# Pair 0's k by keys is transposed on TensorE, and the last 64 positions of k, q and v come in a load of their own

## The chip, the cores and the metric

The kernel runs on one core of one Trainium2 chip. Its time is device microseconds, from the first to the last instruction with what the device adds around them. A core has five engines, each with its own program: TensorE (PE, with its weight loads as PEld), VectorE (DVE), ScalarE (ACT), GpSimd (POOL) and SyncE (SP), which here issues nearly all transfers.

## The reference

Three stages follow each other: retention attention (32 heads, 576 positions, head size 64), a feed-forward layer with hard-swish, and one with SoLU and a layer norm.

```python
scores = scale * np.matmul(q, k.transpose(0, 1, 3, 2))      # (4, 8, 576, 64)
gamma = 1.0 - 2.0 ** (-5.0 - np.arange(H))
Dmat = np.where(rel >= 0, gamma[:, None, None] ** rel[None, :, :], 0.0)
x = np.matmul(scores * Dmat, v)                             # then (2304, 512)
h = x @ w_in                                                # (512, 2048)
x = (h * np.clip(h + 3.0, 0.0, 6.0) / 6.0) @ w_out
h = x @ w2_in                                               # (512, 1024)
e = np.exp(h - h.max(-1)); solu = h * e / (e.sum(-1) + 1e-09)
ln = (solu - mean) / np.sqrt(var + 1e-06) * g_ln
out = ln @ w2_out                                           # (2304, 512)
```

## The kernel before

Attention works on pairs of heads, 16 in all, and within a pair on five chunks: four of 128 positions and a last one of 64. Because the decay is a power of the distance, only the diagonal 128x128 blocks of the scores are computed; everything older goes through a running state per chunk. For pair n the names in the trace are these.

- k and q transposed (head size on the partitions): rk, rq; k by keys (positions on the partitions): rn; v: rv. For the first three pairs all four are called raw (in the order's rows raw0_0 is k of pair 0, raw0_1 q, raw0_2 k by keys, raw0_3 v).
- s: the scores of the four full chunks (`scores`); st: these scaled by ACT and masked by POOL.
- z: the scores of the last 64 positions (`short`); st4: z times mask4, on DVE.
- v: rv scaled by the decay (`prep`), on ACT or DVE.
- u: k by keys times v (`chunk_states`), from which DVE sums the four states (state).
- xp: the output of a pair, from st and v (`values`) and from state and q (`short`); xa: xp times the table tab on DVE (`evac_x`).
- place: one matmul and copies on ACT and POOL that make tab.

In `kernel` the host lays k and q out as 576 columns, the last 64 of them with the two heads swapped, and v as nine rows per partition, of which the last holds the last 64 positions.

The first part of the program, up to the second layer's products, is not written in its final order. Each step is entered in a plan (`Plan`) with its engine, an estimate of its time, what it reads and what it writes. TensorE's steps keep the order in which they are entered. For the others the plan plays the program through, several times, and sets the order in which each engine's steps are issued, by due times and by estimates of engines and transfers (`LOOK`, `DMA_KB`, `HELD` and others); some elementwise steps may go to DVE instead of POOL or ACT. All of SP's transfers form one queue, issued in order.

At the start PE runs warm, nine matmuls on zeros (`N_WARM`), then s of pair 0, z, place, u of pair 0, s of pair 1, xp, z and u of pair 1, and so on. From pair 5 on a share of the first layer, h, stands between the pairs. Transfers of the first three pairs (`EARLY`) use buffers of later stages, those of the other pairs three or four buffers each (`PA`).

Of the kernel before, what the change touches and what calls it, by code (L numbers as in the profile page):

```python
# [9 lines left out]
F32 = mybir.dt.float32  # L10
# [26 lines left out]
WRAW = 2  # L37
EARLY = 3
NE = 4
N_WARM = 9  # L40
PRODUCTS = (
    ("a11", "b11"), ("a12", "b21"), ("s2", "t2"), ("s1", "t1"), ("s4", "b22"), ("s3", "t3"), ("a22", "t4"),
)
# [66 lines left out]
class Plan:  # L110


    LOOK, HOP, DMA_US, DMA_KB, DMA_ONE = 0.8, 0.2, 2.2, 375.0, 150.0
    DEEP, PASSES, YIELD, GAP, KEEP = 3.0, 5, 0.3, 5.0, 1e9
    HELD = ((3.0, 1.4), (23.0, 0.3))

    def __init__(self):
        self.ops, self.homes, self.last = [], {}, {}
# [135 lines left out]
    def simulate(self, nexts, free, loose=False):  # L254
# [51 lines left out]
        while len(begun) < len(self.ops):  # L306
            progress = True
            while progress:
                progress = False
                for e in engines:  # L310
                    if e in active or idle_at[e] > now:
                        continue
                    o = choose(e)
                    if o is None:
                        continue
                    waiting[o.engine].discard(o)
                    if o.engine != e:
                        o.engine, o.us, o.port = "DVE", o.alt[1], True
                    o.start = now
                    begun.append(o)  # L320
                    for v in starts[o]:
                        freed(v, now)
                    if e == "SP":
                        idle_at[e] = now + 0.1
                        begin = max(dma, now)
                        dma = begin + o.kb / self.DMA_KB
                        dma += sum(us for at, us in self.HELD if begin < at <= dma and not loose)
                        o.end = max(dma, now + o.kb / self.DMA_ONE) + self.DMA_US
                        ends.append(o)
# [24 lines left out]


@with_exitstack
def retention_hardswish_solu_kernel(ctx, tc, kt, qt, kn, vt, w1, w2i, w2o, gln, decay, place, out):


    nc = tc.nc  # L360
# [543 lines left out]
    def at_x(c):  # L904

        return slice(128 + CHUNKS[c].start, 128 + CHUNKS[c].stop)

    def load_pair(pr):

        if pr >= NPAIR:  # L910
            return
        early = pr < EARLY
        tag = "wi" if pr < 2 else "g"
        rk, rq, rn, rv = (
            buf("g" if i == 3 else tag, shape, f"raw{pr}_{i}") if early else abuf(name, shape, f"{name}{pr}")
            for i, (name, shape) in enumerate((
                ("rk", [128, S]), ("rq", [128, S + 128]), ("rn", [128, 512]), ("rv", [128, 9, D]),
            ))
        )
        move(288, lambda: sy.dma_start(out=rk(), in_=kt[pr]), (), (rk,))  # L920
        n = S if early else S + 128
        move(n / 2, lambda: sy.dma_start(out=rq()[:, :n], in_=qt[pr][:, :n]), (), ((rq, 0),))
        move(288, lambda: sy.dma_start(out=rv(), in_=vt[pr]), (), (rv,))
        move(256, lambda: sy.dma_start(out=rn(), in_=kn[pr]), (), (rn,))
        for h in range(2 if early else 0):
            def go(e, h=h):
                o, i = rq()[HEADS[h], S:], rq()[HEADS[1 - h], CHUNKS[3]]
# [6 lines left out]
        raws[pr] = rk, rq, rn, rv  # L934

    def prep(pr):

        if pr >= NPAIR:
            return
        rv = raws[pr][3]  # L940
        v = vs[pr] = abuf("v", [128, 9, D], f"v{pr}")
        p = pr % NP
        for i, (c0, n, at) in enumerate(((0, 4, 2 * p), (4, 4, 2 * p + 1), (8, 1, H + NP + p))):
            def go(e, c0=c0, n=n, at=at):
                o, i = (x()[:, c0:c0 + n].rearrange("p c d -> p (c d)") for x in (v, rv))
# [5 lines left out]
            either(0.3 if n > 1 else 0.15, 0.5 if n > 1 else 0.33, go, (rv,), ((v, i),), "ACT").earliest = 5.6  # L951

    def scores(pr):

        sp = [pbuf(f"s{h}", [128, 512], f"s{pr}_{h}") for h in range(2)]
        st = sts[pr] = [abuf(f"st{h}", [128, 512], f"st{pr}_{h}") for h in range(2)]
        k, q, _, _ = raws[pr]
        wide = pr <= A_FROM

        def go():  # L960
# [23 lines left out]
    def short(pr, now, old):  # L984
# [3 lines left out]
        if now:  # L988
            zp = pbuf("z", [128, 64], f"z{pr}")
            st4 = sts4[pr] = abuf("st4", [128, 64], f"st4{pr}")  # L990
            k, q, _, _ = raws[pr]
            reads, writes = [k, (q, 0)], [zp]
        first = pr > A_FROM
        if old:
            if first:
                xps[pr - 1] = pbuf("xp", [128, 1024], f"xp{pr - 1}")
            xp = xps[pr - 1]
            oq, v, state, ost4 = raws.pop(pr - 1)[1], vs[pr - 1], states.pop(pr - 1), sts4.pop(pr - 1)
            reads, writes = [*reads, oq, v, state, ost4], [*writes, xp]
# [536 lines left out]
    now = 0.0  # L1536
# [121 lines left out]
```

## Time and profile before

| | |
|---|---|
| median of 3 runs | 627.79 us (627.13 to 628.36) |
| profiled execution | 627.86 us, span 626.1 us |
| PE busy | 620.6 us, 99% |
| DVE, ACT, POOL busy | 464.2, 398.5, 313.5 us |
| moved by transfers | 145.77 MB, 233 GB/s over the span, 376 GB/s in the first 60 us |

The span is the time from the first to the last instruction; the 1.8 us beside it lie around the program. Busy time is the time in which an engine had an instruction under way. A wait is the idle time of an engine before an instruction, with what ended it behind the arrow. A record of a matmul runs into the next one's, so that start times say more than durations; a plain float32 matmul has two records.

### The profile page before, as it was taken

To read this page: it belongs to the slowest core of one execution; us is meant where nothing else is said; L and a number is where in the kernel's file an instruction comes from. 1 tells how busy PE (TensorE), PEld (TensorE's weight loads), DVE (VectorE), ACT (ScalarE), POOL (GpSimd) and SP (SyncE) were. 2 spreads that over 40 slices of the span, in tenths; PEclk is the share of its full clock that TensorE was granted. 3 is DMA by queue.
4 is the path that set the end of the run, shared out by engine and by line. 5 is a ranking of instruction groups with operands and counts; after the bars stand their busy time and mean duration, and the time that the engine had idled before them with its cause. 6 is when DMAs were issued, how large, how long until landed. Compare 5 with 4: busy or idle time off the path is not lost.

```text
span 626.1 us, 11161 instructions
## 1 busy us (share of the span) xinstructions
PE 620.6 (99%) x3999; PEld 518.6 (83%) x3999; DVE 464.2 (74%) x830; ACT 398.5 (64%) x690; POOL 313.5 (50%) x315
## 2 busy tenths in 40 slices
PE   8999999999999999999999999999999999999997
PEld 5878888988888888888888888888988888888887
DVE  4887999876788785798689888552878868778740
ACT  5887867956667551567566665421676876877672
POOL 6764733304344402572054230542578998999453
PEclk9999999999999999999999999999999999999999
DMA  9999987859667695745998669966665553344441
GB/s 325 394 391 397 408 305 264 294 195 329 203 211 245 209 321 189 294 167 185 379 309 307 222 215 389 383 254 195 175 189 129 118 90 96 102 101 85 84 113 56
DMA packets 91914, 145.77 MB, mean 233 GB/s; under 512 B 43858, under 2 KB 49746, under 8 KB 91860
## 3 DMA queue, kind: packets, MB, share of 16 engines
q1 hardware_dynamic: 91712, 145.06, 69.6%
q8 instruction: 31, 0.51, 0.3%
q14 instruction: 23, 0.19, 0.1%
q10 hardware_dynamic: 148, 0.02, 0.0%
HBM read 92.36 MB, written 43.25 MB: 217 GB/s over the span
## 4 chain that ended last, share of the span: by engine, by line
PE 96%; DMA 3%; SPq 0%; issue 0%; ACT 0%
PE acc L67 29%; PE h L67 23%; PE o L67 16%; PE sd L67 6%; PE sc L67 6%; PE sa L67 6%; PE sb L67 3%; PE xp L67 3%; PE x L67 2%; PE s L67 2%; DMA rn<-in_kn_dram 1%; PE u L67 1%; DMA rk<-in_kt_dram 1%; DMA raw<-in_qt_dram 1%; SPq L67 0%; PE z L67 0%
## 5 line engine op out<-in xcount | busy, mean ns | idle before, releaser
L67 PE MATMUL acc<-g,w1l 128*128 128x512 f32 x624 | 154.1, 389 | 0.0
L67 PEld LDWEIGHTS acc<-g,w1l 128*128 128x128 f32 x624 | 117.1, 188 | 24.3
L67 PE MATMUL o<-w,lt 128*128 128x512 f32 (+1 forms) x456 | 103.0, 378 | 0.0
L67 PEld LDWEIGHTS o<-w,lt 128*128 128x128 f32 x456 | 82.4, 188 | 16.3 <-POOL lt L67 0.4
L67 POOL TENSOR_TENSOR lt<-lT,lt 128x512 fp32r<-128x512 f32 x36 | 61.2, 1719 | 13.4 <-ACT lt L67 13.2
L67 ACT ACTIVATE e<-h,stat 128x1024 f32<-128x1024 f32 x36 | 41.3, 1148 | 35.1 <-DVE stat L67 35.1
L67 PE MATMUL h<-w2t,xt 128*128 128x512 f32 x216 | 53.5, 389 | 0.0
L67 PEld LDWEIGHTS h<-w2t,xt 128*128 128x128 f32 x216 | 40.3, 188 | 8.2
L67 PE MATMUL h<-x,w 128*128 128x512 f32 (+1 forms) x216 | 45.8, 361 | 0.0
L67 PE MATMUL acc<-g,w 128*128 128x512 f32 (+1 forms) x216 | 43.5, 354 | 0.0
L67 PEld LDWEIGHTS acc<-g,w 128*128 128x128 f32 x216 | 36.5, 189 | 6.1
L67 PEld LDWEIGHTS h<-x,w 128*128 128x128 f32 x216 | 34.9, 189 | 7.0 <-issue 1.7
L67 PE MATMUL h<-w2b,xt 128*128 128x512 f32 x162 | 39.8, 390 | 0.0
L67 ACT ACTIVATE wz<-wraw 128x512 f32<-128x512 f32 x44 | 29.4, 668 | 12.9 <-DMA wraw<-in_w2o_dram 5.0
L67 POOL TENSOR_TENSOR g<-gf,g 128x512 fp32r<-128x512 f32 (+1 forms) x18 | 24.1, 1336 | 26.3 <-ACT g L67 26.2
L67 DVE CUSTOM_DVE_ANT_0 wz<-wz,wt 128x1024 uint16<-128x1024 uint16 x44 | 35.2, 801 | 2.3 <-ACT wt L67 1.1
L67 DVE TENSOR_SCALAR e<-h,stat 128x1024 f32<-128x1024 f32 x18 | 20.5, 1142 | 21.0 <-POOL stat L67 21.0
L67 PEld LDWEIGHTS h<-w2b,xt 128*128 128x128 f32 x162 | 30.2, 188 | 6.1
L67 ACT ACTIVATE wt<-wraw 128x512 int32<-128x512 uint32 x48 | 31.9, 664 | 3.4 <-DMA wraw<-in_w2o_dram 1.0
L67 DVE CUSTOM_DVE_ANT_0 h<-h,h 128x512 f32<-128x512 f32 x36 | 24.7, 685 | 11.7 <-PE h L67 4.7
L67 DVE SCALAR_TENSOR_TENSOR h<-h,e 128x1024 f32<-128x1024 f32 x18 | 28.1, 1563 | 7.0 <-ACT e L67 7.0
L67 ACT ACTIVATE g<-gf 128x512 fp32r<-128x512 f32 (+1 forms) x44 | 26.4, 600 | 10.2 <-DVE gf L67 8.9
(193 smaller groups left out, 1359.6 us busy)
## 6 DMA issues: line engine op xcount, KB each, us to landing
w1l<-w1s SPq DMA_DIRECT2D x34, 512.0 KB, 6.0
wraw<-in_w_dram SPq DMA_DIRECT2D x32, 512.0 KB, 5.7
w1s<-w1o SPq DMA_DIRECT2D x10, 512.0 KB, 4.5
x2l<-x2s SPq DMA_DIRECT2D x18, 256.0 KB, 5.9
x2f<-x2o SPq DMA_DIRECT2D x18, 256.0 KB, 5.1
x2r<-x2f SPq DMA_DIRECT2D x9, 512.0 KB, 4.6
rq<-in_qt_dram SPq DMA_DIRECT2D x13, 352.0 KB, 6.5
out_dram<-osb SPq DMA_DIRECT2D x17, 256.0 KB, 2.0
```

Source lines behind the costliest of these rows:

```text
L67: return lambda *args, **kw: self.keep(op(*args, **kw))
```

## The change

The host no longer puts the last 64 positions at the end of k, q and v. They form an array of their own, rt, with 192 columns per pair: k, q and v of those positions. Each pair has one more load, of 96 KB, and its other loads have 256 or 320 KB instead of 288 or 352. z and the last chunk's part of xp read rt.

For pair 0 the load of k by keys goes. In its place PE transposes the four chunks of k by matmuls against a unit matrix, eye, into one bank (flip), and a copy on DVE or ACT brings it to the buffer that u reads. eye is made on POOL by a memset and two selects. The warm-up has six matmuls instead of nine, and three estimates of the plan are others.

```diff
-N_WARM = 9
+N_WARM = 6
...
-    HELD = ((3.0, 1.4), (23.0, 0.3))
+    HELD = ((3.0, 0.4), (5.2, 0.4), (12.5, 0.6))
...
-                        o.end = max(dma, now + o.kb / self.DMA_ONE) + self.DMA_US
+                        o.end = max(dma, now + o.kb / self.DMA_ONE if now > self.FRESH else 0.0) + self.DMA_US
...
+    eye = pa.tile([128, 128], F32, name="eye")
...
+    ge.memset(eye, 1.0)
+    for step in (1, -1):
+        ge.affine_select(
+            out=eye, in_=eye, compare_op=ALU.is_ge, fill=0.0, base=0, pattern=[[step, 128]], channel_multiplier=-step,
+        )
...
+    def flip(rk, rn):
+
+        kp = bank("flip", at=0)
+
+        def go():
+            for c in range(4):
+                te.matmul(kp()[:, CHUNKS[c]], rk()[:, CHUNKS[c]], eye, start=(c == 0), stop=(c == 3))
+
+        def copy(e):
+            if e is se:
+                se.activation(out=rn(), in_=kp(), func=ACTF.Copy)
+            else:
+                ve.tensor_copy(out=rn(), in_=kp())
+
+        pl.op("PE", 0.95, go, (rk,), (kp,))
+        either(V_US, A_US, copy, (kp,), (rn,), "ACT")
...
-        move(288, lambda: sy.dma_start(out=rk(), in_=kt[pr]), (), (rk,))
-        n = S if early else S + 128
+        move(256, lambda: sy.dma_start(out=rk(), in_=kt[pr]), (), (rk,))
+        n = 512 if early else 640
         move(n / 2, lambda: sy.dma_start(out=rq()[:, :n], in_=qt[pr][:, :n]), (), ((rq, 0),))
-        move(288, lambda: sy.dma_start(out=rv(), in_=vt[pr]), (), (rv,))
-        move(256, lambda: sy.dma_start(out=rn(), in_=kn[pr]), (), (rn,))
+        move(256, lambda: sy.dma_start(out=rv(), in_=vt[pr]), (), (rv,))
+        rt = abuf("rt", [128, 3, 64], f"rt{pr}")
+        move(96, lambda: sy.dma_start(out=rt(), in_=short_rows[pr]), (), (rt,))
+        if pr:
+            move(256, lambda: sy.dma_start(out=rn(), in_=kn[pr]), (), (rn,))
+        else:
+            flip(rk, rn)
...
-                    te.matmul(zp()[HEADS[h]], k()[HEADS[h], CHUNKS[4]], q()[HEADS[h], CHUNKS[4]], start=True, stop=True)
+                    te.matmul(zp()[HEADS[h]], rt()[HEADS[h], 0], rt()[HEADS[h], 1], start=True, stop=True)
...
-                (2, st[:, 1], rq[:, CHUNKS[2]]), (4, st[:, 3], rq[:, CHUNKS[4]]),
+                (2, st[:, 1], rq[:, CHUNKS[2]]), (4, st[:, 3], ort()[:, 1]),
```

On PE the order stays, but for the start: nine warm matmuls before, six and four flips now, the flips directly ahead of s of pair 0. Behind that, from the last matmul of s of pair 0 to the first of s of pair 1, PE's rows were these.

```order
L67 MATMUL s0_1_199<-raw0_1_169,raw0_0_167 128x128
L67 MATMUL z0_209<-raw0_1_169,raw0_0_167 64x64 x2
L67 MATMUL place_214<-place_row_144 128x512
L67 MATMUL u0_229<-v0_220,raw0_2_175 64x64 x8
L67 MATMUL s1_0_253<-raw1_1_182,raw1_0_179 128x128
```

And now:

```order
L67 MATMUL s0_1_209<-raw0_1_173,raw0_0_171 128x128
L67 MATMUL z0_224<-rt0_177 64x64 x2
L67 MATMUL place_230<-place_row_144 128x512
L67 MATMUL u0_241<-v0_221,raw0_2_217 64x64 x8
L67 MATMUL s1_0_258<-raw1_1_183,raw1_0_179 128x128
```

z reads rt, and u's second operand is the buffer that the copy of flip writes. On DVE, from the copy of a part of q of pair 0 to the first sum of the state of pair 0, the rows were these.

```order
L67 COPY raw0_1_169<-raw0_1_169 64x128
L67 TENSOR_TENSOR st40_218<-z0_209,mask4_149 128x64
L67 TENSOR_SCALAR v0_220<-raw0_3_171,decay_sb_143 128x256
L67 TENSOR_SCALAR v0_220<-raw0_3_171,decay_sb_143 128x64
L67 COPY state0_243<-u0_229 128x64
```

And now:

```order
L67 COPY raw0_1_173<-raw0_1_173 64x128
L67 COPY raw0_2_217<-flip_196 128x512
L67 TENSOR_SCALAR v0_221<-raw0_3_175,decay_sb_143 128x256
L67 TENSOR_TENSOR st40_234<-z0_224,mask4_149 128x64
L67 COPY raw1_1_183<-raw1_1_183 64x128 x2
L67 COPY state0_269<-u0_241 128x64
```

The copy of flip stands ahead of v; the small part of v went to ACT, and the copies of q of pair 1 came from ACT. On SP, the loads up to the ones that pair 4's u and pair 5's s read (kn of pair 4 is rn4, k of pair 5 rk5) were these.

```order
L67 DMA rq4_281<-in_qt_dram 128x704
L67 DMA rn3_302<-in_kn_dram 128x512
L67 DMA rk4_318<-in_kt_dram 128x576
L67 DMA wraw_338<-in_w1_dram 128x1024
L67 DMA rv4_359<-in_vt_dram 128x576
L67 DMA rq5_377<-in_qt_dram 128x704
L67 DMA rn4_397<-in_kn_dram 128x512
L67 DMA rk5_417<-in_kt_dram 128x576
```

And now:

```order
L67 DMA rn3_290<-in_kn_dram 128x512
L67 DMA rq4_313<-in_qt_dram 128x640
L67 DMA rt3_330<-in_rt_dram 128x192
L67 DMA rk4_342<-in_kt_dram 128x512
L67 DMA wraw_353<-in_w1_dram 128x1024
L67 DMA rv4_387<-in_vt_dram 128x512
L67 DMA rn4_400<-in_kn_dram 128x512
L67 DMA rt4_417<-in_rt_dram 128x192
L67 DMA rq5_421<-in_qt_dram 128x640
L67 DMA rk5_444<-in_kt_dram 128x512
```

rt of a pair stands behind rv or rq, and rn4 ahead of rq5 now. The rows of DVE, ACT, POOL and SP differ in places up to the last third of what the plan orders; behind that and in the part that is written out by hand they are the same.

## Rows read from the trace of the kernel before

**Rows 1.** The page: TensorE's busy time, share of the span, instructions.
```profile
PE 620.6 (99%) x3999; PEld 518.6 (83%) x3999; DVE 464.2 (74%) x830; ACT 398.5 (64%) x690; POOL 313.5 (50%) x315
```

**Rows 2.** Waits of PE, whole span: total us, times, longest.
```profile
PE warm L67 <- DVE idle L440: 1.4, 1, 1.4
PE s L67 <- DMA raw<-in_qt_dram: 0.6, 1, 0.6
PE u L67 <- DMA rn<-in_kn_dram: 0.3, 1, 0.3
```

**Rows 3.** Timeline of PE, 0 to 30 us: start, duration, out<-in, records.
```profile
4.96 1.16 PE L67 MATMUL s<-raw,raw 64*128 64x128 f32 x16
6.05 0.33 PE L67 MATMUL z<-raw,raw 64*64 64x64 f32 x4
6.31 1.12 PE L67 MATMUL place<-place_row 2*128 2x512 f32 x2
7.36 0.69 PE L67 MATMUL u<-v,raw 128*64 128x64 f32 x16
8.61 1.16 PE L67 MATMUL s<-raw,raw 64*128 64x128 f32 x16 [0.56 <-DMA raw<-in_qt_dram]
...
21.07 0.27 PE L67 MATMUL z<-rq,rk 64*64 64x64 f32 x1
...
22.17 0.69 PE L67 MATMUL u<-v,rn 128*64 128x64 f32 x16 [0.32 <-DMA rn<-in_kn_dram]
22.87 1.16 PE L67 MATMUL s<-rq,rk 64*128 64x128 f32 x16
```

**Rows 4.** The chain of waits, 0 to 60 us: start, duration, what.
```profile
3.13 5.34 DMA raw<-in_qt_dram
8.49 5.98 DMA rk<-in_kt_dram
14.48 7.55 DMA rn<-in_kn_dram
```

**Rows 5.** Timeline of SP's queue, 0 to 30 us: issue, duration of issuing.
```profile
0.80 0.38 SPq L67 DMA_DIRECT2D raw<-in_kt_dram  x1
...
16.12 0.33 SPq L67 DMA_DIRECT2D rk<-in_kt_dram  x1
...
22.84 0.33 SPq L67 DMA_DIRECT2D rq<-in_qt_dram  x1
```

**Rows 6.** Transfers: 10 to 20, 34 to 44 (two rows), 70 to 80 us.
```profile
DMA packets 1770, 3.97 MB, mean 397 GB/s; under 512 B 197, under 2 KB 197, under 8 KB 1769
...
DMA packets 1971, 3.96 MB, mean 396 GB/s; under 512 B 218, under 2 KB 474, under 8 KB 1969
...
xd<-xa SPq DMA_DIRECT2D x3, 64.0 KB, 5.5
...
DMA packets 1485, 4.07 MB, mean 407 GB/s; under 512 B 295, under 2 KB 591, under 8 KB 1483
```

**Rows 7.** Timeline of PE, short windows from 3.7 to 4.8 us.
```profile
3.48 0.63 PE L67 MATMUL warm<-idle 128*128 128x512 bf16 x1
...
3.91 0.96 PE L67 MATMUL warm<-idle 128*128 128x512 bf16 x3
...
4.27 0.60 PE L67 MATMUL warm<-idle 128*128 128x512 bf16 x2
```

**Rows 8.** Window 3.8 to 4.3 us: busy (records), granted clock, transfers' share, GB/s.
```profile
3.80:4.30 0.50, 0.50 (x3) 1.00 1.08 396
```

**Rows 9.** Transfers issued from 0.7 to 1 us: count, KB, us to landing.
```profile
raw<-in_kt_dram SPq DMA_DIRECT2D x1, 288.0 KB, 2.9
```

**Rows 10.** Timeline of POOL, 0 to 8 us.
```profile
0.80 1.44 POOL L443 MEMSET mask<- 64x64 f32 x8 [0.29 <-POOLq L1647]
2.32 0.90 POOL L445 TENSOR_SCALAR_AFFINE_SELECT mask<-mask 64x256 f32<-64x256 f32 x2
```

**Rows 11.** Timeline of DVE, 4 to 13 us.
```profile
4.84 0.22 DVE L67 COPY raw<-raw 64x128 f32<-64x128 f32 x1 [3.52 <-DMA raw<-in_qt_dram]
...
11.65 0.76 DVE L67 TENSOR_TENSOR xa<-xp,tab_sb 128x576 f32<-128x576 f32 x1 [1.74 <-PE xp L67]
```

More of the change, by code (lines that the diff above doesn't have):

```diff
@@ L110 @@
 class Plan:
-    LOOK, HOP, DMA_US, DMA_KB, DMA_ONE = 0.8, 0.2, 2.2, 375.0, 150.0
+    LOOK, HOP, DMA_US, DMA_KB, DMA_ONE, FRESH = 0.8, 0.2, 2.2, 375.0, 150.0, 2.0
     DEEP, PASSES, YIELD, GAP, KEEP = 3.0, 5, 0.3, 5.0, 1e9
-    HELD = ((3.0, 1.4), (23.0, 0.3))
+    HELD = ((3.0, 0.4), (5.2, 0.4), (12.5, 0.6))
     def __init__(self):
@@ L356, in retention_hardswish_solu_kernel @@
 @with_exitstack
-def retention_hardswish_solu_kernel(ctx, tc, kt, qt, kn, vt, w1, w2i, w2o, gln, decay, place, out):
+def retention_hardswish_solu_kernel(ctx, tc, kt, qt, kn, vt, short_rows, w1, w2i, w2o, gln, decay, place, out):
     nc = tc.nc
@@ L895, in retention_hardswish_solu_kernel @@
     idle_b = known("x2e", idle)
-    PA = {"rk": 3, "rq": 4, "rn": 3, "rv": 3, "v": 3, "st0": 2, "st1": 2, "state": 2, "st4": 2, "xa": 2}
+    PA = {"rk": 3, "rq": 4, "rn": 3, "rv": 3, "rt": 4, "v": 3, "st0": 2, "st1": 2, "state": 2, "st4": 2, "xa": 2}
     def abuf(tag, shape, name):
@@ L914, in load_pair @@
         rk, rq, rn, rv = (
-            buf("g" if i == 3 else tag, shape, f"raw{pr}_{i}") if early else abuf(name, shape, f"{name}{pr}")
+            buf("gf" if not pr and i == 2 else "g" if i == 3 else tag, shape, f"raw{pr}_{i}") if early else abuf(name, shape, f"{name}{pr}")
             for i, (name, shape) in enumerate((
-                ("rk", [128, S]), ("rq", [128, S + 128]), ("rn", [128, 512]), ("rv", [128, 9, D]),
+                ("rk", [128, 512]), ("rq", [128, 640]), ("rn", [128, 512]), ("rv", [128, 8, D]),
             ))
         )
-        move(288, lambda: sy.dma_start(out=rk(), in_=kt[pr]), (), (rk,))
-        n = S if early else S + 128
+        move(256, lambda: sy.dma_start(out=rk(), in_=kt[pr]), (), (rk,))
+        n = 512 if early else 640
         move(n / 2, lambda: sy.dma_start(out=rq()[:, :n], in_=qt[pr][:, :n]), (), ((rq, 0),))
-        move(288, lambda: sy.dma_start(out=rv(), in_=vt[pr]), (), (rv,))
-        move(256, lambda: sy.dma_start(out=rn(), in_=kn[pr]), (), (rn,))
+        move(256, lambda: sy.dma_start(out=rv(), in_=vt[pr]), (), (rv,))
[5 more added lines that the diff above has]
+            flip(rk, rn)
         for h in range(2 if early else 0):
             def go(e, h=h):
-                o, i = rq()[HEADS[h], S:], rq()[HEADS[1 - h], CHUNKS[3]]
+                o, i = rq()[HEADS[h], 512:], rq()[HEADS[1 - h], CHUNKS[3]]
                 if e is se:
@@ L933, in load_pair @@
             either(0.22, 0.28, go, ((rq, 0),), ((rq, 1 + h),), "ACT")
-        raws[pr] = rk, rq, rn, rv
+        raws[pr] = rk, rq, rn, rv, rt
     def prep(pr):
@@ L939, in prep @@
             return
-        rv = raws[pr][3]
+        _, _, _, rv, rt = raws[pr]
         v = vs[pr] = abuf("v", [128, 9, D], f"v{pr}")
@@ L944, in go @@
             def go(e, c0=c0, n=n, at=at):
-                o, i = (x()[:, c0:c0 + n].rearrange("p c d -> p (c d)") for x in (v, rv))
+                o = v()[:, c0:c0 + n].rearrange("p c d -> p (c d)")
+                i = rv()[:, c0:c0 + n].rearrange("p c d -> p (c d)") if n > 1 else rt()[:, 2]
                 if e is se:
@@ L949, in go @@
                     ve.tensor_scalar(out=o, in0=i, scalar1=decay_sb[:, at:at + 1], scalar2=None, op0=ALU.mult)
-            either(0.3 if n > 1 else 0.15, 0.5 if n > 1 else 0.33, go, (rv,), ((v, i),), "ACT").earliest = 5.6
+            either(0.3 if n > 1 else 0.15, 0.5 if n > 1 else 0.33, go, (rv if n > 1 else rt,), ((v, i),), "ACT").earliest = 5.6
     def scores(pr):
@@ L956, in scores @@
         st = sts[pr] = [abuf(f"st{h}", [128, 512], f"st{pr}_{h}") for h in range(2)]
-        k, q, _, _ = raws[pr]
+        k, q = raws[pr][:2]
         wide = pr <= A_FROM
@@ L990, in short @@
             st4 = sts4[pr] = abuf("st4", [128, 64], f"st4{pr}")
-            k, q, _, _ = raws[pr]
-            reads, writes = [k, (q, 0)], [zp]
+            rt = raws[pr][4]
+            reads, writes = [rt], [zp]
         first = pr > A_FROM
@@ L997, in short @@
             xp = xps[pr - 1]
-            oq, v, state, ost4 = raws.pop(pr - 1)[1], vs[pr - 1], states.pop(pr - 1), sts4.pop(pr - 1)
-            reads, writes = [*reads, oq, v, state, ost4], [*writes, xp]
+            (_, oq, _, _, ort), v, state, ost4 = raws.pop(pr - 1), vs[pr - 1], states.pop(pr - 1), sts4.pop(pr - 1)
+            reads, writes = [*reads, oq, ort, v, state, ost4], [*writes, xp]
         def go():
@@ L1010, in go @@
             for c, w, qc in (
-                (1, st[:, 0], rq[:, CHUNKS[1]]), (3, st[:, 2], rq[:, S:]),
-                (2, st[:, 1], rq[:, CHUNKS[2]]), (4, st[:, 3], rq[:, CHUNKS[4]]),
+                (1, st[:, 0], rq[:, CHUNKS[1]]), (3, st[:, 2], rq[:, 512:]),
+                (2, st[:, 1], rq[:, CHUNKS[2]]), (4, st[:, 3], ort()[:, 1]),
             ):
@@ L1602, in retention_hardswish_solu_kernel @@
     pb.release()
-_INS = ["kt", "qt", "kn", "vt", "w1", "w2i", "w2o", "gln", "decay", "place"]
+_INS = ["kt", "qt", "kn", "vt", "rt", "w1", "w2i", "w2o", "gln", "decay", "place"]
 def kernel(**inputs):
@@ L1614 @@
     kt, qt = (np.array(a.transpose(0, 2, 1).reshape(NPAIR, 2 * D, S)) for a in (k, q))
-    for a in (kt, qt):
-        a[:, :, 512:] = np.roll(a[:, :, 512:], D, axis=1)
-    qt = np.concatenate([qt, np.roll(qt[:, :, 384:512], D, axis=1)], axis=2)
+    rt = np.empty((NPAIR, 128, 3, 64), np.float32)
+    for i, a in enumerate((kt, qt)):
+        rt[:, :, i] = np.roll(a[:, :, 512:], D, axis=1)
+    kt, qt = kt[:, :, :512], np.concatenate([qt[:, :, :512], np.roll(qt[:, :, 384:512], D, axis=1)], axis=2)
     kn = k[:, :512].reshape(NPAIR, 2, 4, 128, D).transpose(0, 3, 2, 1, 4).reshape(NPAIR, 128, 512)
-    vt = np.empty((NPAIR, 128, 9, D), np.float32)
-    vt[:, :, :8] = v[:, :512].reshape(NPAIR, 2, 4, 128, D).transpose(0, 3, 1, 2, 4).reshape(NPAIR, 128, 8, D)
+    vt = v[:, :512].reshape(NPAIR, 2, 4, 128, D).transpose(0, 3, 1, 2, 4).reshape(NPAIR, 128, 8, D)
     for h in range(2):
-        vt[:, 64 * h:64 * h + 64, 8] = v[1 - h::2, 512:]
+        rt[:, 64 * h:64 * h + 64, 2] = v[1 - h::2, 512:]
     wi, wo, w2i, w2o = (
@@ L1644 @@
     place, decay = place.astype(np.float32), np.concatenate([over, step, last, np.roll(step, D, axis=0)], axis=1).astype(np.float32)
-    host = dict(kt=kt, qt=qt, kn=kn, vt=vt, w1=w1, w2i=w2i, w2o=w2o, gln=gln, decay=decay, place=place)
+    host = dict(kt=kt, qt=qt, kn=kn, vt=vt, rt=rt, w1=w1, w2i=w2i, w2o=w2o, gln=gln, decay=decay, place=place)
     nc = _bacc.Bacc("TRN2", target_bir_lowering=False, num_devices=1, dynamic_dma_scratch_size=1024)
```

## The prediction

> **What bounds the kernel now.** I read the page first: TensorE (PE) is busy 620.6 of 626.1 us [rows 1]. Then PE's waits over the whole span: three in all, 1.38 us before the first warm-up matmul, 0.56 us for pair 1's q and 0.32 us for pair 4's k by keys [rows 2]. So after about 23 us PE never waits, and whatever happens to the other engines later can only add time. The change can win inside the first 23 us alone, and there at most 0.56 + 0.32 = 0.88 us, unless the first score matmul itself starts sooner. The timeline of PE places both waits: s of pair 1 starts at 8.61; u of pair 4 stands directly before s of pair 5, which starts at 22.87 [rows 3].
>
> The chain of waits says what feeds PE there: transfers, 3.13 to 8.47, 8.49 to 14.47, 14.48 to 22.03, one behind the other [rows 4]. Each link begins when the link before it has landed. The order shows why: eight loads stand between the two, and SP does not issue a load before the one eight places ahead has landed. By the same count the landing of rk5 (pair 5's k) is bounded: the load eight places behind it, rq7, is issued at 22.84 [rows 5]. So s of pair 5, at 22.87, starts just when rk5 is there: the transfers and PE meet at that place, although no wait is shown. From there each pair also carries a share of h on PE, and PE falls behind the transfers.
>
> **The load of kn for pair 0 goes; the last 64 positions travel alone.** Up to rk5 the queue carries, before, three pairs of 1,120 KB, two of 1,184, wraw with 512, rq5 with 352 and rk5 with 288: 6,880 KB. After: 864 (pair 0) + 2 x 1,120 + 2 x 1,184 + 512 + 320 + 256 = 6,560 KB. 320 KB less at 397 GB/s [rows 6] is 0.83 us. Against it stand four more loads (five of rt, less one of kn). Each is 128 rows and, by the counts of packets, 16 more: 576 packets over 16 engines, 36 each. What a packet costs beside its bytes the trace gives only between bounds. Ten microseconds with 1,770 packets move 3.97 MB, ten with 1,485 move 4.07 MB: solved for a price per packet that is 12 ns. But ten with 1,971 packets, three 64-KB stores among them, move as much as those with 1,770: that makes it nothing [rows 6]. I take the middle, 6 ns: 36 x 6 = 0.22 us, between 0 and 0.43. The transfers thus let s of pair 5 start 0.83 - 0.22 = 0.61 us sooner (0.40 to 0.83), at 22.26.
>
> The new loads are waited for at z, which now reads rt. rt4 has 5,984 KB ahead of it and in it, against 6,592 for kn of pair 4, which landed at 22.03 [rows 4]: 608 KB, 1.57 us sooner, with the packets 20.7. z of pair 4 stands at 21.07 [rows 3] and would be due at 20.70 without waits (21.07 - 0.56 + 0.19, below). It just arrives; a tenth late here only takes the place of the wait at s of pair 5, since xp, u and s are queued behind z. kn of pair 4 itself is now issued ahead of rq5: 5,888 KB, 20.5 us, so its 0.32 us go.
>
> **The first pair.** Six warm-ups instead of nine. The sixth starts at 3.48, the seventh at 3.91, 0.43 us later; the eighth at 4.27, 0.36 later, and the last two are over at 4.87 [rows 7], where at 0.43 us apart the ninth would only start at 4.79. So PE ran at half its later pace until part of the way through the seventh: t at 0.43 us a matmul, the rest at half of that, t + (1 - t/0.43) x 0.215 = 0.36, t = 0.29. The rise lies near 4.20: the 1.2 GHz level before it and 2.4 behind it, by this pace; the granted clock reads 1.00 there [rows 8]. The engine had run back to back since 1.38.
>
> The six end at 3.91. k of pair 0 landed at 0.80 + 2.9 = 3.7 [rows 5, 9] and is 32 KB smaller now, so flip starts at 3.91. The trace has no full 128x128 matmul in plain float32. Low end: place streams 512 columns in 1.05 us (6.31 to 7.36), four flips stream as many. High end: u, K of 128 as in flip, takes 0.69 us for eight of 64 columns, which is half the columns: 1.38. Nearest is s, weights of 128 columns and moving rows of 128, two heads beside each other on half the array: four rounds in 1.09 us (4.96 to 6.05) [rows 3]. I take 1.09. Of it 0.29 us pass at half pace (0.145 done), the rest ends at 4.20 + 0.945 = 5.15. q of pair 0 had landed at 4.84 [rows 11] and brings 64 KB less with it. So flip, not q, releases s: 5.15 instead of 4.96, 0.19 us lost (0.15 to 0.48). The three warm-ups removed cost and give nothing: they lay in the wait for q.
>
> eye comes from POOL: eight memsets of 0.18 and two selects of 0.45 stood at 0.80 to 3.22 [rows 10]; now a memset and two smaller selects stand among the mask's. By those prices eye is complete near 0.80 + 1.44 + 0.2 + 0.9 = 3.3, ahead of 3.91; mask4 follows by 4.3, and z, whose product it masks, starts at 6.05. Were eye late, flip and all behind it would be late by as much. The copy of flip stands on DVE ahead of v and st4: xa, also out of PSUM, is 0.76 us for 576 columns [rows 11], so the copy ends near 5.15 + 0.75 = 5.9, and v's half, 256 columns out of SBUF, takes no longer: 6.65 at the latest. u starts at 7.36 + 0.19 = 7.55, covered by s, z and place. v of pair 1 moves from DVE to ACT, behind st of pair 0 and the copy of place; it is wanted only after s and xp that follow 8.61, so it is covered as well.
>
> q of pair 1 lands 320 KB sooner, 8.47 - 0.83 = 7.6 [rows 4]; PE gets there at 7.36 + 0.69 + 0.19 = 8.24. The 0.56 us go entirely.
>
> **The sum.** PE without waits reaches s of pair 5 at 22.87 - 0.88 + 0.19 = 22.18 (22.14 to 22.47), the transfers at 22.26. The later one counts: 0.61 us won, and carried to the end, because PE's order and amount of work are the same behind it. The profiled execution took 627.86 us, 0.07 above the median of the three runs shown; 627.86 - 0.61 = 627.25, on the scale of the median 627.2. What remains is late at s of pair 5: rk5, 0.08 us.
>
> **Rivals.** (1) The packets cost nothing: the transfers would allow 22.04, PE 22.18, 0.69 us won, 627.1. For it speaks the stretch with 1,971 packets, against it the one with 1,485.
>
> (2) The clock rises late. The three warm-ups ran across 4.20; flip is there now. If flip did not count as the work that raises the clock, it would run 3.91 to 6.09 at half pace, and the rise would come as much later, at 6.38. Loss (6.38 - 4.20) / 2 = 1.09 us; s of pair 5 at 23.27 instead of 22.87, the total 0.40 us slower: 628.2. It decides from a rise after 4.20 + 2 x 0.69 = 5.6 us on. Against it: PE has no gap before or behind flip, and flip is an ordinary matmul by the identity. The Trainium skill, page "TensorE: Matmul & The Clock Gate", section "Part 4: PE-mode transpose", says that a transposition in that mode does not count as PE-busy. By that rule the time would be the 628.2 of this rival; the diff sets no such mode, and no run here shows one.
>
> (3) A small load costs as much as its neighbour of 256 KB. Then five rt add 5 x 160 KB = 800 KB, 2.06 us: the transfers bring s of pair 5 at 22.87 - 0.83 + 2.06 = 24.1, 1.2 us later than before: 629.0; from 0.42 us for an rt on, instead of 0.25, the win is gone (627.8). Against it: three 64-KB stores lie in a stretch that still moved 3.96 MB in ten microseconds [rows 6]. The Trainium skill, page "DMA: Bandwidth & Descriptors", section "Bandwidth", calls transfers under 64 KB descriptor-dominated and shows 64 KB alone taking 0.95 us. By that an rt alone would cost more than a microsecond, as an estimate; here eight loads are under way at once, and the trace shows no such price for the 64-KB stores.
>
> (4) The other engines' order is made anew up to about 400 us, the steps of DVE, ACT and POOL among them. A step set too late would give PE a wait it doesn't have now; nothing bounds it in the rows but that there is none today. I price it like the larger wait of today, 0.6 us, or two of them: 627.8 to 628.4.
>
> **How the numbers follow.** Forecast 0.62 (627.0 to 627.5); rival 1 0.15; rival 2 0.10; rival 3 0.08; rival 4 0.05. A measurement of this kernel tells nothing under 0.2%, 1.26 us, from no change. A win beyond that would need more than the 0.88 us of waits that there are, so faster gets 0.06, for the spread of the runs (627.13 to 628.36) and what I did not see. Slower by over 0.2% is over 629.05: the far end of rival 3, a rise of the clock later than I priced, several waits of rival 4: 0.08. Within: 0.86. The range reaches from rival 1 less the spread of runs to rival 2: 626.6 to 628.3.
>
> **What would show it.** flip starts at 3.9 and s of pair 0 near 5.15; s of pair 1 without a wait, near 8.2; no wait at u of pair 4; s of pair 5 near 22.3, with at most 0.3 us of waits in front of it or of z; none after. A start of s of pair 0 after 5.6 would be rival 2, s of pair 5 after 22.9 rival 3, a wait behind 26 us rival 4.

## The result, and the profile after

The changed kernel takes 631.31 us (median of 7 runs, 630.09 to 634.59); the kernel before took 628.01 beside it (7 runs, 627.13 to 628.79). The ratio as it was estimated (not the quotient of the two medians) is 1.0058, 95% interval 1.0041 to 1.0075: slower by 0.6%, outside the predicted range. The profiled execution took 632.41 us, span 630.7, 4.6 us longer than that of before.

TensorE (PE) again fills its span; the line of the page that answers to [rows 1]:

```profile
PE 623.0 (99%) x4004; PEld 520.4 (83%) x4004; DVE 468.7 (74%) x839; ACT 399.0 (63%) x691; POOL 301.0 (48%) x309
```

PE's waits over the whole span, to be held against [rows 2]:

```profile
PE xp L67 <- DVE xa L67: 2.7, 5, 0.9
PE warm L67 <- DVE idle L441: 1.4, 1, 1.4
PE xp L67 <- DVE st L67: 0.4, 1, 0.4
PE u L67 <- DMA rv<-in_vt_dram: 0.2, 1, 0.2
```

The two waits that the prediction wanted to win are gone. In their place xp waits for VectorE's xa, which it never did before: the bank of xp is single, and xa empties it. The timeline of PE places the waits; its first eight rows answer to [rows 3]:

```profile
3.91 1.92 PE L67 MATMUL flip<-eye,raw 128*128 128x128 f32 x8
5.75 1.55 PE L67 MATMUL s<-raw,raw 64*128 64x128 f32 x16
7.23 0.33 PE L67 MATMUL z<-rt 64*64 64x64 f32 x4
7.49 1.12 PE L67 MATMUL place<-place_row 2*128 2x512 f32 x2
8.54 0.69 PE L67 MATMUL u<-v,raw 128*64 128x64 f32 x16
9.16 1.05 PE L67 MATMUL s<-raw,raw 64*128 64x128 f32 x14
...
22.32 0.69 PE L67 MATMUL u<-v,rn 128*64 128x64 f32 x16
22.94 1.24 PE L67 MATMUL s<-rq,rk 64*128 64x128 f32 x16
...
29.42 0.24 PE L67 MATMUL xp<-st,v 64*64 64x64 f32 x1 [0.27 <-DVE xa L67]
...
49.54 0.27 PE L67 MATMUL xp<-st,v 64*64 64x64 f32 x1 [0.58 <-DVE xa L67]
...
50.49 0.69 PE L67 MATMUL u<-v,rn 128*64 128x64 f32 x16 [0.16 <-DMA rv<-in_vt_dram]
...
55.35 0.27 PE L67 MATMUL xp<-st,v 64*64 64x64 f32 x1 [0.67 <-DVE xa L67]
```

s of pair 5 starts at 22.94, 0.07 us later than before. s of pair 15, the last, starts at 73.68, before at 69.90: 3.78 later; the last matmul of xp starts at 80.8, before at 76.0: 4.8 later, and behind that nothing more is lost. So the loss arises between 23 and 81 us, where the prediction had nothing. Of the ten steps from s of one pair to s of the next, five are 0.5 to 1.05 us longer, the other five as long as before within 0.1 us.

What stands behind xa is seen on DVE, from 46 to 50 us:

```profile
46.80 0.52 DVE L67 TENSOR_SCALAR v<-rt,decay_sb 128x64 f32<-128x64 f32 x1 [1.71 <-DMA rt<-in_rt_dram]
47.24 0.21 DVE L67 TENSOR_TENSOR st<-z,mask 128x64 f32<-128x64 f32 x1
47.37 0.21 DVE L67 COPY state<-u 128x64 f32<-128x64 f32 x1
47.61 1.21 DVE L67 SCALAR_TENSOR_TENSOR state<-state,decay_sb,u 128x64 f32<-128x64 f32 x4
48.74 0.75 DVE L67 TENSOR_TENSOR xa<-xp,tab_sb 128x576 f32<-128x576 f32 x1
```

DVE waits 1.71 us for an rt, the state sums and xa are queued behind, and PE's xp at 49.54 is late by 0.58. A transfer is late, then. The transfers of 12 to 62 us, before the change:

```profile
DMA packets 9022, 19.68 MB, mean 394 GB/s; under 512 B 1000, under 2 KB 1512, under 8 KB 9010
```

And after it:

```profile
DMA packets 9769, 17.58 MB, mean 352 GB/s; under 512 B 1082, under 2 KB 3043, under 8 KB 9757
...
rt<-in_rt_dram SPq DMA_DIRECT2D x11, 96.0 KB, 5.4
```

The rate fell by 11% although each pair asks for no more bytes than before, and a 96-KB rt took 5.4 us to land, about as long as a load of 256 KB (medians of 5.5 to 5.9). The chain of waits, answering to [rows 4], again runs from load to load:

```profile
10.76 6.71 DMA rq<-in_qt_dram
17.48 0.33 SPq L67
17.86 5.59 DMA rv<-in_vt_dram
23.46 6.05 DMA wraw<-in_w_dram
29.58 6.00 DMA rv<-in_vt_dram
35.60 0.35 DVE v L67
```

And SP's queue between two links of it. Its first row, the load eight places behind rk5, answers to the last of [rows 5]:

```profile
22.85 0.33 SPq L67 DMA_DIRECT2D rt<-in_rt_dram  x1
23.46 0.33 SPq L67 DMA_DIRECT2D wraw<-in_w_dram  x1
24.18 0.33 SPq L67 DMA_DIRECT2D rq<-in_qt_dram  x1
24.56 0.42 SPq L67 DMA_DIRECT2D rk<-in_kt_dram  x1
25.27 0.33 SPq L67 DMA_DIRECT2D rv<-in_vt_dram  x1
25.93 0.33 SPq L67 DMA_DIRECT2D rn<-in_kn_dram  x1
26.55 0.42 SPq L67 DMA_DIRECT2D rt<-in_rt_dram  x1
27.30 0.33 SPq L67 DMA_DIRECT2D rq<-in_qt_dram  x1
27.68 1.01 SPq L67 DMA_DIRECT2D rk<-in_kt_dram  x1
29.58 0.33 SPq L67 DMA_DIRECT2D rv<-in_vt_dram  x1
```

By the prediction's own count rk5 had thus landed just before 22.85, as before (22.84), although 320 KB less stood ahead of it: the four more loads had taken back the whole 0.83 us.

wraw, issued at 23.46, lands at 29.51, and the last row, eight places behind it, is issued at 29.58. Eight loads are under way, and the rt among them holds one of the eight places. That gave the theory: **slots**. A load costs its place, whatever its size, since the bytes under way are eight times the mean load. (SP also takes 0.25 to 0.43 us for most issues, so that a load may pay by being issued; the experiments count loads and don't separate the two.) Rivals: **head of line** (DVE's v waiting for rt holds up xa), **packets** (the 768-byte pieces cost engine time beside their bytes: solving the two rows above as the prediction solved its own gives some 50 ns a packet; the expectations below took 30), **clock** (PE started at half pace until about 6.5 us; the prediction had 4.2), **order** (any plan made anew is worse than the one before).

### The profile page after: what moved, and what is told of

It reads as the page before. It is cut to its first block, busy times and chain, and to the rows that moved or that the text cites. A ratio compares the mean times of both kernels' runs of the same rounds, so it can differ in the third digit from the quotient of the medians.

```text
span 630.7 us, 11206 instructions
## 1 busy us (share of the span) xinstructions
PE 623.0 (99%) x4004; PEld 520.4 (83%) x4004; DVE 468.7 (74%) x839; ACT 399.0 (63%) x691; POOL 301.0 (48%) x309
## 4 chain that ended last, share of the span: by engine, by line
PE 87%; DMA 9%; DVE 3%; issue 0%; SPq 0%; ACT 0%; DVEq 0%; ACTq 0%
PE acc L67 29%; PE h L67 20%; PE o L67 16%; PE sd L67 6%; PE sc L67 6%; PE sa L67 6%; PE sb L67 3%; PE x L67 2%; DMA rv<-in_vt_dram 2%; DMA wraw<-in_w_dram 2%; DMA rt<-in_rt_dram 2%; DMA rq<-in_qt_dram 1%; DMA rn<-in_kn_dram 1%; DVE state L67 1%; DMA raw<-in_qt_dram 1%; DMA raw<-in_vt_dram 1%
## 5 line engine op out<-in xcount | busy, mean ns | idle before, releaser
L67 DVE CUSTOM_DVE_ANT_0 wz<-wz,wt 128x1024 uint16<-128x1024 uint16 x44 | 38.2, 869 | 2.3 <-ACT wt L67 0.6
L67 POOL TENSOR_TENSOR w1f_s<-ws,w1f_s 128x512 fp32r<-128x512 f32 x13 | 17.3, 1336 | 43.7 <-ACT w1f_s L67 43.7
L67 DVE SCALAR_TENSOR_TENSOR h<-h,e 128x1024 f32<-128x1024 f32 x18 | 31.0, 1723 | 6.4 <-ACT e L67 6.4
L67 POOL TENSOR_SCALAR_AFFINE_SELECT st<-st 128x512 f32<-128x512 f32 x32 | 20.8, 672 | 26.6 <-ACT st L67 26.5
```

The lines of the kernel that those rows point to most:

```text
L67: return lambda *args, **kw: self.keep(op(*args, **kw))
```

## The experiments

Each kernel was timed 4 to 12 times, beside the kernel before on the same chip. The numbers side by side first. s 5 and s 15 are the starts of s of pairs 5 and 15, and loads is what SP issued from 12 to 62 us, stores included (8 of the 62 before). These and the rate are of one profiled execution, which is not always near the median: it took 628.30 us against 630.20 in a_two_strided, 632.31 against 629.82 in a_two_packed, 628.20 against 629.24 in a_four.

| kernel | ratio (95%) | s 5 | s 15 | GB/s, 12 to 62 us | loads |
|---|---|---|---|---|---|
| before | 1 | 22.87 | 69.90 | 394 | 62 |
| after | 1.0058 (1.0041 to 1.0075) | 22.94 | 73.68 | 352 | 68 |
| b_rt: before + rt loads | 1.0101 (1.0082 to 1.0119) | 23.08 | 73.43 | 362 | 67 |
| b_flip6: before + flip | 1.0031 (1.0018 to 1.0044) | 22.89 | 70.82 | 391 | 61 |
| b_const: before + estimates | 1.0028 (1.0017 to 1.0039) | 22.78 | 71.48 | 390 | 62 |
| a_warm8: after, 8 warm | 1.0076 (1.0054 to 1.0099) | 22.68 | 72.13 | 368 | 71 |
| a_two_strided: 8 loads of rt | 1.0021 (1.0008 to 1.0035) | 22.93 | 70.67 | 382 | 67 |
| a_two_packed: 8, half the packets | 1.0026 (1.0009 to 1.0042) | 23.05 | 71.90 | 371 | 66 |
| a_vfree: v not from rt | 1.0056 (1.0041 to 1.0071) | 23.23 | 73.07 | 357 | 68 |
| b_warm6: before, 6 warm | 1.0021 (1.0007 to 1.0034) | 26.66 | 73.75 | 366 | 59 |
| a_four: 4 loads of rt | 1.0018 (1.0000 to 1.0035) | 22.94 | 70.50 | 386 | 64 |
| a_four_warm8 | 1.0012 (1.0003 to 1.0021) | 23.03 | 70.64 | 380 | 64 |
| b_tiny1: before + 16 loads of 64 B | 1.0099 (1.0084 to 1.0115) | 23.10 | 73.83 | 347 | 69 |
| b_tiny128: before + 16 of 8 KB | 1.0100 (1.0086 to 1.0114) | 23.50 | 74.63 | 347 | 68 |

**One part at a time.** b_rt is before with the rt loads and z, v and xp reading them; k by keys of pair 0 is loaded, the warm-ups are nine and the plan's estimates as before.

```diff
+        rt = abuf("rt", [128, 3, 64], f"rt{pr}")
+        move(96, lambda: sy.dma_start(out=rt(), in_=short_rows[pr]), (), (rt,))
```

> The kernel before with one part of the change: the last 64 positions of k, q and v in a load of their own. Pair 0's k by keys is loaded, nine warm-ups, the plan's constants as before. Theory A (the small loads: five loads a pair instead of four lower the transfers' rate from 394 to about 352 GB/s between 12 and 62 us, v and rt come late, DVE stands still before v, xa behind it is late, PE waits at xp): slower, 630 to 632 us, at least 1.5 us of waits of PE at xp after 26 us and under 370 GB/s in that stretch. Theory B (the clock rises about 2.3 us later because flip stands where three warm-ups were, and PE runs out of step with the plan from there): the clock rises near 4.2 as before, 627.5 to 628.5 us. Theory C (the plan's new constants make a worse order): 627.5 to 628.5 us, since the constants are the old ones.

b_flip6 is before with flip and six warm-ups, no rt, estimates as before.

```diff
-N_WARM = 9
+N_WARM = 6
...
-        move(256, lambda: sy.dma_start(out=rn(), in_=kn[pr]), (), (rn,))
+        if pr:
+            move(256, lambda: sy.dma_start(out=rn(), in_=kn[pr]), (), (rn,))
+        else:
+            flip(rk, rn)
```

> The kernel before with the other part: pair 0's k by keys made by flip on TensorE, six warm-ups, no load of it; k, q and v keep 576 columns, the plan's constants as before. Theory A (small loads): the transfers keep 390 GB/s or more, no wait at xp, and 256 KB less: 627.0 to 628.2 us. Theory B (late clock): s of pair 0 starts near 5.8 and takes 1.5 us, as in the changed kernel, and the total is 629.5 to 632 us. Theory C (constants): 627.0 to 628.2 us.

b_const is before with the changed estimates of the plan alone (`HELD`, and the condition with `FRESH`), which only order other engines' steps anew.

```diff
-    HELD = ((3.0, 1.4), (23.0, 0.3))
+    HELD = ((3.0, 0.4), (5.2, 0.4), (12.5, 0.6))
...
-                        o.end = max(dma, now + o.kb / self.DMA_ONE) + self.DMA_US
+                        o.end = max(dma, now + o.kb / self.DMA_ONE if now > self.FRESH else 0.0) + self.DMA_US
```

> The kernel before, with nothing but the plan's new constants (HELD and FRESH): the same loads and steps, in another order. Theory C (the constants make a worse order): 629.5 to 632 us with waits of PE after 26 us. Theories A and B: 627.3 to 628.7 us, PE without a wait after 26 us.

b_rt lost 1.0%, more than the whole change and more than theory A said (634.26 us); each of the others lost 0.3%, at 390 GB/s. b_flip6 came out where theory B had put it, with s of pair 0 at 5.91, but the late clock is not its loss: s of pair 5 starts at 22.89, as before, and behind that xp waits 0.60 us for DVE's st, at 29.70. b_const waits at such places too (0.36 us for POOL's w at 27.72), as theory C said. So the small loads are the main part, and a new order costs something by itself.

**The start.** a_warm8 is the changed kernel, in its order, with eight warm-ups.

```diff
-N_WARM = 6
+N_WARM = 8
```

> The changed kernel with eight warm-ups instead of six, entered in the plan with the same total, so that every other engine has the same order. Theory B (late clock): the clock rises near 4.2, before flip; flip starts at 4.5 and takes 1.1 us, s of pair 1 starts near 8.6 instead of 9.16, PE is in step with the plan again and the total falls to 627.3 to 628.5 us. Theory A (small loads): the start is 0.5 us earlier, but the transfers set the pace up to 80 us, the waits at xp grow by what the start wins: 630 to 632 us. Theory C (constants): as A, 630 to 632 us.

PE's timeline of a_warm8 at the start:

```profile
1.38 3.26 PE L67 MATMUL warm<-idle 128*128 128x512 bf16 x8 [1.38 <-DVE idle L441]
4.47 1.05 PE L67 MATMUL flip<-eye,raw 128*128 128x128 f32 x8
5.46 1.16 PE L67 MATMUL s<-raw,raw 64*128 64x128 f32 x16
```

flip runs at full pace (0.99 us from start to start, before s) and s of pair 1 starts at 8.47 instead of 9.16. The time is no better, and s of pair 15 is still 2.2 us late: the early start is lost again in waits for xa (2.0 us). The clock is not where the time went. b_const shows more: there nine warm-ups stand as in the kernel before, and no flip, and yet PE's timeline is

```profile
1.38 4.02 PE L67 MATMUL warm<-idle 128*128 128x512 bf16 x9 [1.38 <-DVE idle L440]
5.33 1.57 PE L67 MATMUL s<-raw,raw 64*128 64x128 f32 x16
```

s took 1.57 us where it had 1.16 [rows 3]. The rise came late here without any flip.

b_warm6 is before with six warm-ups, its order on every engine otherwise untouched.

```diff
-N_WARM = 9
+N_WARM = 6
```

> The kernel before with six warm-up matmuls in place of nine, and nothing else: the order on every engine is as before, no rt loads, k by keys still loaded. Theory order (the 0.3% of the kernel with the flip alone, 1.0031, and of the one with new constants alone, 1.0028, is the price of an order made anew): ratio 0.999 to 1.001. Rival clock (fewer warm-ups leave the first matmuls at half pace, and that stays in the end): s of the first pair starts at 4 to 4.4 us and takes about 2 us rather than 1.09, and the time is 0.5 to 1 us longer: 1.001 to 1.002.

PE's timeline of b_warm6:

```profile
5.20 2.08 PE L67 MATMUL s<-raw,raw 64*128 64x128 f32 x16 [1.09 <-DMA raw<-in_qt_dram]
...
9.61 1.12 PE L67 MATMUL u<-v,raw 128*64 128x64 f32 x16
10.66 2.08 PE L67 MATMUL s<-raw,raw 64*128 64x128 f32 x16
...
15.71 0.69 PE L67 MATMUL u<-v,raw 128*64 128x64 f32 x16
16.33 1.16 PE L67 MATMUL s<-raw,raw 64*128 64x128 f32 x16
```

The clock theory was right for this kernel, and by far more than I had put down: with no flip to fill the gap PE stood idle for 1.09 us and then ran at half pace until about 15 us. s of pair 2 is 4.28 us late (16.33 against 12.05), s of pair 15 3.85; nothing more is lost behind the start, and no wait is left there. So this kernel says nothing on the order. Its 12 runs reach from 627.30 to 631.78, as if the start differed between executions; only one of them was profiled.

**Slots or packets.** In a_two_strided, whose edit stands here, one load brings the rt of two pairs; in a_two_packed the two also lie side by side in memory, so that there are half as many packets. All other instructions stand in the changed kernel's order.

```diff
-        move(96, lambda: sy.dma_start(out=rt(), in_=short_rows[pr]), (), (rt,))
...
+            if pr % 2 == 0:
+                t = pa.tile([128, 2, 3, 64], F32, tag="rt2", bufs=3, name=f"rt2_{pr}")
+                rts[pr].tile, rts[pr + 1].tile = t[:, 0], t[:, 1]
+                sy.dma_start(out=t, in_=short_rows[pr:pr + 2].rearrange("r p a d -> p r a d"))
```

> The changed kernel with the last 64 positions of two pairs in one load: 8 loads of 192 KB in place of 16 of 96 KB, still in pieces of 768 bytes (256 packets a load, as many packets and bytes in all). The order on all engines is the changed kernel's; only every second small load is gone from SP. Theory slots (a load costs its place among the eight in flight and its issue, whatever its size): four loads a pair and a half in place of five, so most of the loss of 0.58% goes: ratio 1.001 to 1.003, transfers of 12 to 62 us at 375 GB/s or more, waits of xp for xa under 1.5 us. Theory packets (each of the 768-byte pieces costs some 30 ns of engine time beside its bytes): nothing is gained, ratio 1.005 to 1.008, 350 to 365 GB/s, xp waits for xa 2 us or more.

In the packed one the source is `short_rows[pr // 2]`.

> As the strided one, but with the two pairs side by side in memory: 8 loads of 192 KB in pieces of 1536 bytes, 128 packets a load, so half the small loads and half their packets. Theory slots: the same as the strided one, ratio 1.001 to 1.003. Theory packets: the loss is about halved here and not there: 1.002 to 1.004 against 1.005 to 1.008, 370 to 380 GB/s against 350 to 365. If the loss came neither from loads nor packets but from the new order, both are at 1.005 or more.

Half the loads took away more than half of the loss, with all the packets left (1.0021) as with half of them (1.0026). Packets fall. The profiled execution of a_two_packed, near the longest of its twelve, missed what slots had it at: 371 GB/s, and 1.9 us of waits for xa.

**Head of line.** In a_vfree the third scaling reads rv.

```diff
-                i = rv()[:, c0:c0 + n].rearrange("p c d -> p (c d)") if n > 1 else rt()[:, 2]
+                i = rv()[:, c0:c0 + n].rearrange("p c d -> p (c d)") if n > 1 else rv()[:, 0]
```

> The changed kernel, same order on all engines and same transfers, but the scaling that makes v's last 64 positions reads rv, landed earlier, in place of rt (so the last 64 positions of v are left out of what is computed; z and xp still read rt). Theory head of line (VectorE's scaling waits for rt, the evacuation xa stands behind it, TensorE waits for xa): VectorE's waits for rt (4.5 us in the changed kernel) are gone, TensorE's waits of xp for xa fall from 2.7 us to under 1 us, ratio 1.001 to 1.004. Rival bandwidth (the transfers are late as a whole): the waits come back elsewhere, as VectorE waiting for rv, or TensorE's u, s or z for rv, rk or rt by 2 us or more in all, ratio 1.005 to 1.007.

DVE's waits in a_vfree, 12 to 62 us:

```profile
DVE xa L67 <- DMA xd<-xa: 4.3, 4, 2.0
DVE xa L67 <- PE xp L67: 2.6, 2, 1.4
```

DVE's waits for rt are gone, and nothing is won: xa now waits for the store of an earlier xa, which stands in the same queue. PE waits for xa 2.3 us all the same. Taking away the one late transfer that DVE stood at gained nothing while the others stayed late. My first theory of the place falls with this: v behind rt is where the lateness is met, not its cause.

**The price of a load by itself.** b_tiny1 is before, in its order on every engine, with a load of 64 bytes behind each load of rv, which nothing reads. b_tiny128 has 128 rows of 64 bytes in it.

```diff
+            sy.dma_start(out=pa.tile([1, 16], F32, tag="tiny", bufs=16, name="tiny"), in_=decay[:1, :16])
```

> The kernel before, with its order on every engine, and behind each of the 16 loads of v one more load of 64 bytes (one row of 16 numbers, one packet), which nothing reads. Bytes and packets are nothing. Theory slots: a load costs its place among the eight in flight, or its issue on SP, so that five loads a pair instead of four bring the transfers of 12 to 62 us from 394 GB/s to 370 or less, waits of xp for xa appear behind 26 us, ratio 1.003 to 1.010. Rival size (the cost of the small loads lies in their bytes, rows and packets, or in the kernel's new order): 0.999 to 1.001.

> As the one with 64-byte loads, but each of the added loads has 128 rows of 64 bytes (8 KB, 128 packets, as many as a load of rt). Theory slots: within 0.2% of the one with a single row. Theory packets (some 30 ns of engine time a packet, so 128 over 16 engines cost 0.24 us a load and 3.8 us in all where the transfers bound): here 1.003 to 1.008, and with a single row 0.999 to 1.001.

The transfers of b_tiny1, 12 to 62 us:

```profile
DMA packets 8065, 17.37 MB, mean 347 GB/s; under 512 B 916, under 2 KB 1428, under 8 KB 8053
...
tiny<-in_decay_dram SPq DMA_DIRECT2D x12, 0.1 KB
```

And PE's waits of it:

```profile
PE xp L67 <- DVE xa L67: 2.9, 6, 0.6
```

Sixteen loads that bring a kilobyte in all cost 634.14 - 628.37 = 5.8 us, 0.36 us each, with about the same waits for xa as in the changed kernel. Those of 8 KB cost as much (6.1 us); but in the one execution profiled of them 2.03 us are a single wait for xa, which ended at 45.66, and some 1.7 more, as an estimate, the half pace of PE behind it: the granted clock reads 0.50 from 46 to 48 us. b_rt's loads of 96 KB cost 634.26 - 628.16 = 6.1 us, in an order of its own. So what is paid for is the load: 64 bytes in one packet are enough.

Whether it pays by its place or by its issue is not shown. From 12 to 62 us SP spent 24.1 us issuing before, 27.0 in b_tiny1 and 31.2 in the changed kernel (the sums of its rows), so that it was not short of time as a whole; but single issues took up to 2.06 us in the changed kernel, and a place that came free meanwhile stood empty.

**Fewer still.** a_four brings the rt of four pairs in a load, a_four_warm8 the same with eight warm-ups.

```diff
+            if pr % 4 == 0:
+                t = pa.tile([128, 4, 3, 64], F32, tag="rt4", bufs=2, name=f"rt4_{pr}")
...
+                sy.dma_start(out=t, in_=short_rows[pr // 4])
```

> The changed kernel with the last 64 positions of four pairs in one load: 4 loads of 384 KB in place of 16 of 96 KB, the order on all engines otherwise the changed kernel's. Theory slots (each load holds one of eight places in flight, whatever its size): 16 small loads gave 1.0058, 8 gave 1.0021 and 1.0026, so 4 give 1.000 to 1.002, with less than 1 us of TensorE's waits for VectorE's xa behind 26 us and 385 GB/s or more from 12 to 62 us. Rival order (what is left at 8 loads, 0.2%, is the price of the new order, not of loads): 1.002 to 1.003 again, with waits that have no late transfer behind them.

> The one with four pairs' last positions in a load, with eight warm-up matmuls in place of six, same order. With sixteen small loads eight warm-ups gave nothing (1.0076 against 1.0058), because the transfers, not the start, set the time. Theory slots: with only 4 such loads the start counts again; flip at full pace, s of the first pair at 5.5 rather than 5.8 us, and 0.3 us less than the kernel with six: 0.999 to 1.001. Rival: the start wins nothing here either, and the two are equal within their intervals.

Transfers of a_four, 12 to 62 us:

```profile
DMA packets 9304, 19.32 MB, mean 386 GB/s; under 512 B 1034, under 2 KB 1546, under 8 KB 9292
...
rt<-in_rt_dram SPq DMA_DIRECT2D x3, 384.0 KB, 6.1
```

Four loads give most of the rate back, and one wait of xp for xa is left (0.3 us), in the shortest of its eleven executions. The time is within 0.2% of before by the estimate; a_four_warm8 can't be told from a_four, as the rival had it; its profile doesn't test the start, since its eight warm-ups, at half pace for longer, end only at 4.76 us, and z then waits 0.37 us for the first rt. What is left, 0.1 to 0.2%, is no more than b_const and b_flip6 showed for a new order; it was not taken apart. Nor was the difference between b_rt (1.0101) and the whole change (1.0058), which differ in flip, the warm-ups and the estimates, so the parts don't add up. No version beat the kernel before: there were 0.88 us to win [rows 2], 0.14%, less than these runs tell apart.

## Why the prediction was wrong

**The step that failed** is the one from 23 us on: "whatever happens to the other engines later can only add time", and then nothing was added, since "from there [...] PE falls behind the transfers". It rested on PE showing no wait there [rows 2]. For what PE reads itself that was true: k of pair 8 landed at 33.26 and its s started at 37.23, and from pair 6 on k and q landed 2 to 5 us before s, in both kernels. But xp also needs the bank that xa empties, and the engines that make v had no time in hand, before the change too. These are rows of ACT in the kernel before:

```profile
26.69 1.15 ACT L67 ACTIVATE v<-rv,decay_sb 128x256 f32<-128x256 f32 x3 [0.23 <-DMA rv<-in_vt_dram]
...
31.03 0.51 ACT L67 ACTIVATE v<-rv,decay_sb 128x256 f32<-128x256 f32 x1 [0.72 <-DMA rv<-in_vt_dram]
```

v of pairs 5 to 9 was begun within 0.2 us of the landing of rv. A load that lands later holds up DVE or ACT, the steps queued behind, and through xa PE.

Nor could the queue catch up. From 12 to 62 us SP issued 62 transfers of 307.6 KB on average, one every 0.81 us, and eight of them at a landing of 6.4 us (the mean of the views' medians) make 8 x 315 kB / 6.4 us = 394 GB/s, which is the rate shown. The sum itself says only that eight were under way all the time. That SP went as fast as the places let it is in the landings: of 54 transfers for which the trace has the landing of the one eight places ahead, 45 were issued within 0.1 us of it. With rt the mean load is 255.5 KB and lands in 5.7 us: 365 by the same sum, 352 shown, and only 33 of 59 were issued that promptly; at 32.38 SP took 2.06 us to issue an rt. The prediction named the eight places, used them to find which load comes when, and then priced loads by their bytes and packets.

**The term mis-sized** is the price of the small loads: 0.22 us for four, 0.055 each, by packets [rows 6]. Ahead of pair 5 the four took the whole 0.83 us, 0.2 each, if nothing else in the new order cost time there; over the whole kernel a load without bytes cost 0.36 (b_tiny1), and there were sixteen. The rows that gave between 0 and 12 ns a packet were stretches with few small loads among large ones, where the mean load changes little.

**The rivals.** Rival 3 had the price nearly right: 0.66 us for 256 KB [rows 6] is 0.41 us beside the 0.25 of an rt's own bytes, and 0.36 was measured. I gave it 0.08, and priced it up to pair 5 only, where it would have made s start at 24.1; s started at 22.94. Over sixteen loads it makes 6.6 us, near b_rt's 6.1. Against it I set three 64-KB stores in a stretch that kept its rate: they stand in the queue as often before the change as after it, and two loads of 512 KB stood beside them. Rival 4, a new order, is real: 1.8 us in b_const, and as much in b_flip6, more than the 0.6 to 1.2 us of waits that I gave it. Rival 2 came in with its symptom, not its reason: s of pair 0 at 5.75, where from 5.6 on it should decide. But the rise was as late in b_const, without flip, and early in both a_two kernels, with flip; where it came early in the changed order (a_warm8) nothing was won. When it came was luck, as far as the runs show.

**What held.** flip starts at 3.91 as computed; at full pace it takes 0.99 us where I took 1.09. The waits for q of pair 1 and for k by keys of pair 4 are gone. They paid for the late clock: s of pair 1 at 9.16 instead of the predicted 8.24, s of pair 5 at 22.94 instead of 22.26, both 0.7 to 0.9 us late, a little less than half pace until about 6.5 rather than 4.2 costs by the prediction's count (2.3 / 2 = 1.15 us, of which flip's shorter time gives 0.1 back). With an early clock 22.26 would have been missed too, since rk5 was not there: in a_warm8 s of pair 5 starts at 22.68, after 0.2 us of waiting for rk.

## What to carry to other kernels

Where a queue has a fixed number of loads under way and issues the next one the moment a place comes free, count loads and not bytes alone: a load split off costs something even if it has 64 bytes. Put small inputs of several steps into one load. And before calling a stretch free because the busy engine shows no wait, look at the waits of the engines that feed it: if one of them starts each step as its load lands, a later load reaches the busy engine through it.

## What the runs showed of the hardware

- In a queue of loads of 256 to 512 KB with eight transfers under way, one more load of 64 bytes cost 0.36 us (b_tiny1). The landing of a load hardly shrank with its size: 5.3 us for the 8 KB of b_tiny128, 5.4 for an rt of 96 KB, 5.5 for 192 KB, 6.1 for 384 KB.
- The rise of TensorE's clock comes at different times in different executions of the same start. With six warm-ups, flip started at 3.91 us in every kernel of the changed order, and s of pair 0 behind it at 5.02 (a_two_strided), 5.03 (a_two_packed), 5.42 (a_vfree), 5.75 (after) or 5.76 us (a_four): flip took between 1.11 and 1.85 us. The predicted 5.15 lies among them. With nine warm-ups and no flip s of pair 0 took 1.16 us (before) or 1.57 (b_const).
- The granted clock reads 1.00 in all of these stretches, and the pace of the matmuls shows which of the two levels it was. The traces' own lists of clock changes begin with the rise, at 4.19 us before (the prediction worked out 4.20), 6.22 in b_const and 6.60 after.
- In b_warm6, where PE stood idle for 1.09 us behind six warm-ups, half pace lasted until about 15 us. In b_tiny128, where PE stood idle for 2.03 us until 45.66, the granted clock fell, and reads 0.50 from 46 to 48 us.
